# State products of the later pairs, moved directly behind their transposes in a chunked scan fused with a feed-forward block

## The chip, the cores and the metric

The kernel runs on one core of one Trainium2 chip. The metric is the device time of one execution in microseconds (us), the median over several executions. Most executions of one kernel agree within a few tenths of a per cent. In the traces the engines are PE (TensorE's matmuls), PEld (its weight loads), DVE (VectorE), ACT (ScalarE), POOL (GpSimd) and SP (the queue that issues DMAs).

## The reference

Two blocks, one after the other, all in FP32. The first is a chunked state-space scan over 4 batches x 8 heads x 768 positions with head dimension 32 and state dimension 16; the second is a feed-forward block of width 2048 with a learned slope for negative values.

```python
for c in range(nc):                                    # chunks of a sequence
    L = np.exp(cum[..., :, None] - cum[..., None, :]) * causal
    M = np.einsum('bhin,bhjn->bhij', Cc, Bc) * L
    y_intra = np.einsum('bhij,bhjd->bhid', M, xc)
    y_inter = np.einsum('bhin,bhnd->bhid', Cc, state) * decay_to_i[..., None]
    y[:, :, sl] = y_intra + y_inter
    state = decay_full * state + (sum over j of B x x, decayed from j to the end)
...
h = x @ w_in                                           # (3072, 256) @ (256, 2048)
g = np.maximum(h, 0.0) + alpha * np.minimum(h, 0.0)
out = g @ w_out
```

## The kernel before

The 24 chunks of 128 positions are worked as 12 "pairs" and six "groups" of 512 tokens. A generator, `pair(gp)`, does the scan of one pair, and every `yield` ends a step that the caller may place where it likes. Pairs 4 to 11 are the "fine" ones: their steps are laid between the products of the feed-forward block of the group before.

```python
    # pair(gp), fine pairs only; cuts are marked
    tp = ss_tile()                                  # one of 2 PSUM buffers
    ... four transposes of B and C into tp; ACT copies bh; DVE makes cd ...
    yield                                           # step 1
    for w in range(2):
        spread_c(range(2 * w, 2 * w + 2))           # ACT: two scaled copies of C
        half_decays(0, w)                           # DVE: two scans
        yield                                       # steps 2, 3
    ... state products: nk x 2 matmuls in 128x64 tiles; DVE: new state; POOL: mask ...
    yield                                           # step 4
    for w in range(2):
        half_decays(1, w)
        yield                                       # steps 5, 6
    ... two grams (steps 7, 8), then y (step 9) ...
```

The feed-forward block uses a Strassen-like scheme: each "quad" (four per group) has seven half-size products of the first layer and, interleaved, the seven products of the second layer of the quad before. `after(j)` marks 14 places inside a quad. ScalarE and VectorE turn each first-layer result into activations.

```python
    first(A, lambda q: wi[:, q, 0, 0], b11, True);  nc.scalar.copy(out=m1, in_=A);  after(1)
    first(Y, lambda q: s1[:, q], t1, True);         nc.scalar.copy(out=m5, in_=Y);  after(2); after(3)
    first(A, lambda q: s2[:, q], t2);               nc.scalar.copy(out=u2, in_=A);  after(4)
    nc.vector.tensor_tensor(out=Y, in0=Y, in1=u2, op=ALU.add);  after(5)
    first(A, lambda q: wi[:, q, 1, 0], t3)
    ...
    prelu(g12, Y, z, 0);  nc.scalar.copy(out=Y, in_=m1);  prelu(g22, c22, z, 1)
    after(7); after(8); after(9)
    ...
    first(A, lambda q: wi[:, q, 1, 1], t4);  prelu(g21, A, z, 1)   # frees A for the next quad
    after(10); after(11)
    first(Y, lambda q: wi[:, q, 0, 1], b21);  prelu(g11, Y, z, 0)
    ... after(12); after(13); after(14)

# (quad z, place j): which pair's next step goes there, the nearer one (0) or the one after (1)
steps = {(0, 1): 0, (0, 2): 0, (0, 3): 0, (0, 9): 0, (0, 14): 0,
         (1, 1): 0, (1, 2): 0, (1, 5): 0, (1, 9): 0,
         (1, 14): 1, (2, 1): 1, (2, 2): 1, (2, 3): 1, (2, 9): 1, (2, 14): 1,
         (3, 1): 1, (3, 3): 1, (3, 7): 1}
```

In the very first quad there are no second-layer products to interleave; only the last outputs of the phase before stand at its places 3 to 9.

## Time and profile before

| | before |
|---|---|
| median of 3 runs | 404.32 us (404.29 to 404.81) |
| TensorE busy in the profiled run | 378.4 of 402.8 us |
| mean granted TensorE clock | 0.996 of full speed |
| TensorE waits over 0.5 us after 101 us | one for VectorE (1.7), one for ScalarE (1.0) |

One line of the page was not looked at in the prediction and turns out to matter. It gives, for 40 equal slices of the span, the clock that the throttle granted to TensorE, in tenths (9 is nine tenths or more):

```profile
PEclk9999999999999999999999999999999999999998
```

The beginning is not covered: the view counts the clock as whole where it holds no record of it. TensorE's first four transposes, at 7.5 to 8.2 us, take 421 to 474 ns each, the later ones from 19.7 us on 272 to 273, so the clock was probably still low at the start.

### The profile page before, as it was taken

Reading aid. Unit: us, or ns where it says so; the run is one execution under the profiler, and the core shown is the slowest. Engines: PE = TensorE matmul, PEld = TensorE weight load, DVE = VectorE, ACT = ScalarE, POOL = GpSimd, SP = SyncE. Lnnn points to the kernel's source line nnn. Section 1 sums busy time; section 2 is a strip of 40 time slices with the busy share of each in tenths; the row PEclk is TensorE's granted clock in tenths of the full one; section 3 lists DMA queues with packets and bytes.
Section 4 is the critical chain, followed back from the end, with each engine's and each line's share of the span. In section 5 each row is a group of like instructions: output and inputs, shape, how many; then the busy total and the mean of one; then the engine's idle time right before and its main releaser. Section 6 shows DMA issues by size and latency. Waiting matters only on the chain.

```text
span 402.8 us, 6008 instructions
## 1 busy us (share of the span) xinstructions
PE 378.4 (94%) x2131; PEld 294.5 (73%) x2131; DVE 255.4 (63%) x493; ACT 180.2 (45%) x409; POOL 192.6 (48%) x188
## 2 busy tenths in 40 slices
PE   5878979999989999999999999999999999999993
PEld 4454638778858867877868878868878868888883
DVE  5889895691775573675764685674586574355363
ACT  3574823522444534554445544434534534534540
POOL 3164674578174954462453471453471454355511
PEclk9999999999999999999999999999999999999998
DMA  8939997100591430100791100891100200003003
GB/s 208 243 113 223 306 189 160 40 20 0 93 206 52 96 75 2 52 0 2 111 194 35 54 1 2 126 185 29 53 2 4 50 0 2 0 0 55 1 2 52
DMA packets 124126, 30.58 MB, mean 76 GB/s; under 512 B 96880, under 2 KB 120000, under 8 KB 124096
## 3 DMA queue, kind: packets, MB, share of 16 engines
q1 hardware_dynamic: 117792, 29.67, 33.2%
q10 hardware_dynamic: 6304, 0.52, 1.1%
q8 instruction: 17, 0.28, 0.3%
q14 instruction: 13, 0.11, 0.1%
HBM read 26.85 MB, written 3.34 MB: 75 GB/s over the span
## 4 chain that ended last, share of the span: by engine, by line
PE 81%; DVE 9%; ACT 3%; POOL 3%; issue 1%; DMA 1%; DVEq 0%; ACTq 0%; POOLq 0%
PE hp L620 30%; PE bank L595 29%; PE bank L537 6%; PE ss L478 5%; PE hp L524 4%; DVE dec L373 2%; PE ss L501 2%; ACT gt L603 1%; DVE wr L227 1%; DVE dec L483 1%; PE ss L407 1%; PE ss L447 1%; DVE gt L528 1%; POOL gt L663 1%; PE ss L494 1%
## 5 line engine op out<-in xcount | busy, mean ns | idle before, releaser
L663 POOL TENSOR_TENSOR gt<-gt 128x512 f32<-128x512 f32 x58 | 73.6, 1269 | 29.5 <-DVE gt L605 12.8
L595 PE MATMUL bank<-gt,w_out 128*128 128x256 f32 x320 | 82.1, 380 | 0.0
L605 DVE SCALAR_TENSOR_TENSOR gt<-hp,s_mul,gt 128x256 f32<-128x256 f32 x120 | 51.8, 477 | 44.8 <-ACT gt L603 41.7
L603 ACT ACTIVATE gt<-hp,s_alpha 128x256 f32<-128x256 f32 x120 | 50.0, 469 | 62.6 <-PE hp L620 61.3
L595 PEld LDWEIGHTS bank<-gt,w_out 128*128 128x128 f32 x320 | 60.3, 190 | 11.3 <-issue 2.3
L595 PE MATMUL bank<-gt,ws 128*128 128x256 f32 x240 | 58.9, 381 | 0.0
L654 POOL TENSOR_TENSOR gt<-gt 128x512 f32<-128x512 f32 x20 | 25.4, 1270 | 64.4 <-DVE gt L605 64.4
L595 PEld LDWEIGHTS bank<-gt,ws 128*128 128x128 f32 x240 | 45.2, 190 | 6.7 <-issue 0.8
L620 PE MATMUL hp<-xs,w_in 128*128 128x256 f32 x160 | 43.6, 395 | 0.5
L620 PE MATMUL hp<-xT,w_in 128*128 128x256 f32 x160 | 41.5, 382 | 1.7 <-DVE gt L605 1.7
L620 PE MATMUL hp<-xs,ws 128*128 128x256 f32 x160 | 42.3, 387 | 0.0
L379 DVE TENSOR_TENSOR_SCAN dec<-abc,bank 128x256 f32<-128x256 f32 x64 | 39.0, 665 | 0.0
L620 PEld LDWEIGHTS hp<-xs,w_in 128*128 128x128 f32 x160 | 28.1, 189 | 11.9 <-issue 5.9
L620 PEld LDWEIGHTS hp<-xs,ws 128*128 128x128 f32 x160 | 29.1, 190 | 10.1 <-issue 3.7
L620 PEld LDWEIGHTS hp<-xT,w_in 128*128 128x128 f32 x160 | 29.7, 190 | 6.7 <-DVE gt L605 3.1
L483 DVE TENSOR_TENSOR dec<-ss,dec 128x512 f32<-128x512 f32 x40 | 25.6, 682 | 10.5 <-PE ss L478 10.5
L605 DVE SCALAR_TENSOR_TENSOR gt<-c,s_mul,gt 128x256 f32<-128x256 f32 x40 | 17.7, 483 | 23.0 <-ACT gt L603 23.0
L537 PE MATMUL bank<-w_out,gt 128*128 128x256 f32 x128 | 30.4, 379 | 0.0
L524 PE MATMUL hp<-xT,w_in 128*128 128x256 f32 x96 | 25.7, 390 | 4.4 <-DVE gt L528 4.4
L639 DVE TENSOR_TENSOR hp<-hp,u 128x512 f32<-128x512 f32 x20 | 14.0, 700 | 21.7 <-ACT u L637 21.4
L537 PEld LDWEIGHTS bank<-w_out,gt 128*128 128x128 f32 x128 | 24.3, 190 | 3.3
L462 POOL TENSOR_TENSOR sm<-state,bmask 128x256 f32<-128x256 f32 (+1 forms) x12 | 7.7, 643 | 39.1 <-DVE state L458 39.1
(122 smaller groups left out, 539.0 us busy)
## 6 DMA issues: line engine op xcount, KB each, us to landing
abc<-z SPq DMA_DIRECT2D x20, 512.0 KB
raw<-in_moe_w_in_dram SPq DMA_DIRECT2D x8, 512.0 KB
raw<-in_moe_w_out_dram SPq DMA_DIRECT2D x8, 512.0 KB
xt<-in_x_dram SPq DMA_DIRECT2D x24, 128.0 KB
out_dram<-o_sb SPq DMA_DIRECT2D x34, 64.0 KB
nat<-in_B_dram SPq DMA_DIRECT2D x22, 64.0 KB
nat<-in_C_dram SPq DMA_DIRECT2D x22, 64.0 KB
ap<-pf SPq DMA_DIRECT2D x10, 128.0 KB
```

The source lines that it names most:

```text
L379: nc.vector.tensor_tensor_scan(out=dv[:, k, hs], data0=abc[k][:, hs], data1=ident_p[0], initial=0.0, op0=ALU.mult, op1=ALU.add)
L478: nc.tensor.matmul(gram[r].rearrange("p h t -> p (h t)"), bh[rs, k], cz[rs, :, k], start=True, stop=True, tile_position=(64 * r, 0), skip_ ...
L483: nc.vector.tensor_tensor(out=dec[:, k, hs], in0=gram[r], in1=dec[:, k, hs], op=ALU.mult)
L524: nc.tensor.matmul(hp, w_in[:, k, f * P : (f + 1) * P], xts[g][:, k, t0 : t0 + nt], start=(k == 0), stop=(k == KC - 1))
L537: nc.tensor.matmul(pos[0][t // 2][:, t % 2], gt[:, t * Q : (t + 1) * Q], w_out[:, f], start=(f == 0 and t % 2 == 0), stop=(f == NF - 1), s ...
L595: nc.tensor.matmul(ms[g][i][:, h], w, blocks[g, z][n][:, p], start=(q == 0 and h == 0), stop=(q == NQ - 1), skip_group_check=True)
L603: nc.scalar.mul(o[:, p], h[:, p], s_alpha[:, fs[p]])
L605: nc.vector.scalar_tensor_tensor(out=o[:, p], in0=h[:, p], scalar=s_mul[:, fs[p]], in1=o[:, p], op0=ALU.mult, op1=ALU.max)
L620: nc.tensor.matmul(to[:, p], w(2 * z + p), b, start=start and p == 0, stop=True, skip_group_check=True)
L639: nc.vector.tensor_tensor(out=Y, in0=Y, in1=u2, op=ALU.add)
L654: nc.gpsimd.tensor_tensor(out=tc_, in0=g22, in1=g12, op=ALU.subtract)
L663: eng.tensor_tensor(out=o, in0=x0, in1=x1, op=ALU.subtract)
```

## The change

The intent: a fine pair's state products are issued directly behind its transposes, so that the small matmuls of a pair interrupt the block products in one place instead of two. Since that removes one step, each pair has one place fewer: (0,3) goes for the first pair of a group, (2,3) for the second. With (0,3) gone, the first pair's second half scans and spreads land at (0,9), where the state products were. Pair 4's scaled B is prepared explicitly in advance.

```diff
         nc.vector.tensor_tensor(out=cd..., in0=ct, in1=pf, op=ALU.mult)
-        yield
-        if fine:
-            for w in range(2):
-                spread_c(range(2 * w, 2 * w + 2))
-                half_decays(0, w)
-                yield
-        elif gp:
+        if not fine:
+            yield
+        if gp and not fine:
             decays(0)
 ...     # state products, then a yield
         if fine:
-            for w in range(2):
-                half_decays(1, w)
-                yield
+            for k in range(2):
+                for w in range(2):
+                    if k == 0:
+                        spread_c(range(2 * w, 2 * w + 2))
+                    half_decays(k, w)
+                    yield
 ...
+    bns[GC] = pair_loads(GC)
 ...
-    steps = {(0, 1): 0, (0, 2): 0, (0, 3): 0, (0, 9): 0, (0, 14): 0,
+    steps = {(0, 1): 0, (0, 2): 0, (0, 9): 0, (0, 14): 0,
 ...
-             (1, 14): 1, (2, 1): 1, (2, 2): 1, (2, 3): 1, (2, 9): 1, (2, 14): 1,
+             (1, 14): 1, (2, 1): 1, (2, 2): 1, (2, 9): 1, (2, 14): 1,
```

## The prediction

> **What bounds the kernel now.** I read the page first, then the waits of TensorE, then the timeline engine by engine around the places that the change touches. Times in timelines are microseconds from the start of the span; the second column is the length, the last word how many records are merged. An FP32 matmul shows as two records.
>
> ```profile
> PE 378.4 (94%) x2131; PEld 294.5 (73%) x2131; DVE 255.4 (63%) x493; ACT 180.2 (45%) x409; POOL 192.6 (48%) x188
> ```
>
> TensorE is the bound. From 101.3 us on (the second phase, 20 "quads" of seven half-size products each, mixed with the state-space work of the later pairs 4 to 11) it hardly rests: over the stretch from 162.08 to 222.00 its busy time is 59.80 of 59.92 us. The wait view has only two TensorE waits over 0.5 us in that phase, one for a copy of ScalarE that the change leaves alone, and this one:
>
> ```profile
> PE hp L620 <- DVE gt L605: 1.7, 1, 1.7
> ```
>
> It sits at 112.6 to 114.3, at the end of the very first quad, where no block products exist yet to fill the time. So a gain must come from TensorE's own order (mode switches, small stalls), and a loss from ScalarE or VectorE being late for it. The timeline of TensorE in the first quad of the third group shows both places of one pair, transposes (L407) and state products (L447):
>
> ```profile
> 162.08 1.03 PE L620 MATMUL hp<-xT,w_in 128*128 128x256 f32 x4
> 162.94 0.60 PE L407 MATMUL ss<-ident,nat 128*128 128x128 f32 x4
> 163.38 1.03 PE L620 MATMUL hp<-xs,ws 128*128 128x256 f32 x4
> ...
> 165.97 1.03 PE L595 MATMUL bank<-gt,w_out 128*128 128x256 f32 x4
> 167.12 1.10 PE L620 MATMUL hp<-xs,w_in 128*128 128x256 f32 x4
> ...
> 168.92 1.89 PE L595 MATMUL bank<-gt,ws 128*128 128x256 f32 x8
> 170.74 0.66 PE L447 MATMUL ss<-xt,bn 128*64 128x128 f32 x8
> 171.33 1.13 PE L620 MATMUL hp<-xs,w_in 128*128 128x256 f32 x4
> 172.29 1.03 PE L595 MATMUL bank<-gt,w_out 128*128 128x256 f32 x4
> ```
>
> Take starts, since ends overlap. A product (x4) takes 0.86 to the next start. The transposes take 163.38 - 162.94 = 0.44 and cost their neighbours nothing (0.86 before them). The state products take 0.59, and in addition the x8 before them takes 1.82 instead of 1.73 (0.09) and the product after them 0.96 instead of 0.86 (0.10): entry, body and exit are 0.78 us. The step 165.97 to 167.12 is 1.15, a stall of 0.29.
>
> **What the Trainium skill says.** "TensorEngine Tiling (Array Packing)", section Tiling Modes, Key Properties: "Changing tiling mode (not just tile) drains the TensorE". The trace agrees: only the 128*64 state products, not the 128*128 transposes, show the 0.09 and 0.10. The transposes are in the products' own mode, so putting the state products behind them takes no switch away. "TensorE: Matmul & The Clock Gate", section Architectural detail: ScalarE and VectorE take their queue strictly in order, and only TensorE pulls weight loads ahead. The trace agrees: below, ScalarE's copy L637 starts only as the spreads L416 end.
>
> **The change part by part.**
>
> (1) State products move from behind places (0,9) and (2,3) to behind the transposes at (0,1) and (1,14), for 8 pairs. Instructions are the same in kind and number. Per pair the entry of 0.09 may shrink behind a short transpose; exit and body remain. I call the entry there E, between 0 and 0.1, and take 0.05: a gain of 0.04 x 8 = 0.3 us. POOL's scaled B (bn) must now be there earlier: for pair 8 it ends at 221.5 and the transposes start at 222.85, for pair 10 at 281.5 against 282.55, so no wait. Pair 4 gets an early call in the code, but before it ran already at 96.67, right behind the same sums. PSUM's two ss buffers are free then (the copies out of the previous pair's y end some 3 us earlier).
>
> (2) In quad 0 of each group, the second pair of half scans and the second two spreads of C move from (0,3) to (0,9). This matters more, for it moves ScalarE's work from before one copy to before another:
>
> ```profile
> 164.93 1.57 ACT L416 ACTIVATE cz<-ss,par 128x256 f32<-128x256 f32 x4
> 166.36 0.61 ACT L637 COPY u<-hp 128x512 f32<-128x512 f32 x1
> ...
> 172.40 0.35 ACT L685 COPY sa<-bank 128x256 f32<-128x256 f32 x1
> 172.65 0.26 ACT L455 COPY state<-ss 128x128 f32<-128x128 f32 x1
> 172.80 0.85 ACT L603 ACTIVATE gt<-hp,s_alpha 128x256 f32<-128x256 f32 x2
> ```
>
> The gain: L637 frees the bank that the product at 167.12 writes; it starts late by about 0.25 because of four spreads. With two of them gone (0.75 us less) the stall of 0.29 goes, in four groups: 1.15 us at most.
>
> The loss: two spreads (some 0.86 us for a pair, the same length as L603 x2) now stand between L685 and L603 at 172.80. L603 is the first half of the activation whose VectorE half frees the bank of the next quad's first product. Offsets from the quad's start (162.08): the products after the moved state products come E + 0.63 later and 0.2 earlier for the stall, so the first activation is at +7.5 + E instead of +7.09; the chain ScalarE, VectorE (0.10 + 0.88), copy, second activation, L685 carries this on to +11.05 + E; two spreads then bring L603 to +11.85 + E (before: 10.72), its end to 12.7 + E, VectorE's end to 12.8 + 0.88 = 13.68 + E, and the next quad's first product to 13.73 + E. Before, it started at 175.75 - 162.08 = 13.67, and by TensorE's own order it could now start at 13.31 + E. The stall of 0.29 that was removed is thus spent again: 0.06 + E, about +0.1 us for each of groups 2 to 4.
>
> (3) In the first group there are no products to hide this. There ScalarE runs two output copies before the activation (111.53 to 112.58), and the wait of 1.72 is its consequence. The same reckoning puts the activation at 113.7 + E instead of 112.47, VectorE's end at 115.5 instead of 114.23, the next quad at 115.5 instead of 114.28: +1.25 us.
>
> (4) What follows in VectorE. Its next work is a line without a gap up to the first gram multiplication:
>
> ```profile
> 175.15 0.88 DVE L605 SCALAR_TENSOR_TENSOR gt<-hp,s_mul,gt 128x256 f32<-128x256 f32 x2 [0.52 <-ACT gt L603]
> ...
> 177.59 2.41 DVE L379 TENSOR_TENSOR_SCAN dec<-abc,bank 128x256 f32<-128x256 f32 x4
> 179.92 1.26 DVE L483 TENSOR_TENSOR dec<-ss,dec 128x512 f32<-128x512 f32 x2
> ```
>
> L483 ends at 181.18 and frees the banks that the second gram takes at 181.41 (the next x4 of L478): a margin of 0.2. L605 moves from +13.07 to +13.68 + E, so L483 ends 0.65 later while TensorE is only 0.1 later: a stall of about 0.3 us in groups 2, 3 and 4, 0.9 in sum. In the first group L483 ends at 118.66 and the second gram comes at 120.05, so nothing is added.
>
> (5) In quad 2 only the state products move (from (2,3) to (1,14)). ScalarE and TensorE there meet as before; the copy L637 was free of the spreads by 0.8 us and is so by nearly nothing now: 0 to 0.1, taken as 0.
>
> Sum: -0.2 (second pairs' entries; the first pairs' are in the E above) + 0.3 + 1.25 + 0.9 = +2.2 us.
>
> **The rivals.** (a) The merge pays: E is 0, exits shrink too, and ScalarE's delay in (2) stays within the slack. Then it is 4 x 0.29 + 8 x 0.09 = 1.9 us less, 402.4, less whatever (3) costs, about 403.6 with it. For it speaks that the change looks like a deliberate tuning step of a kernel where TensorE is full; against it that the transposes need no switch, and that the delay of L603 follows link by link. (b) The scans or spreads at (0,9) fall where VectorE or ScalarE is already late, and each of the four groups loses some 1.2 us as the first does: 404.3 + 5 = 409. Against it speaks the slack of 0.6 us between VectorE's end and the next quad at 175.75. (c) A transfer or bn on POOL becomes the wait behind the transposes: margins of 1.1 to 1.3 us speak against it; each miss would cost some tenths of a microsecond, giving 405 to 407. (d) All moves lie within the slack: 404.3.
>
> **Range and chances.** The sum gives 406.5. I take 0.4 off for rival (a) and get 406.1. The range reaches from (a) with (3), 403.6, to the sum with larger stalls in (2) and (4), 407.9. Two per cent are 8.1 us: all the stalls in the phase sum to less than half of that, so faster by 2% is all but impossible, and slower by 2% needs (b) and more.
>
> **What would show it.** In the trace after: state products right behind transposes with 0.44 + E + 0.59 between starts and 0.96 for the product after them, the same as before (step 1); 0.86 to 0.95 in place of the 1.15 (step 2, gain); the first quad's wait on VectorE grown from 1.7 to about 2.9 (step 3); a new wait of 0.3 to 0.5 before the second quad's first product, and one of about 0.3 before the second gram, in groups 2 to 4. The prediction is wrong if the state products behind transposes take far less than 0.7, or if the first quad's wait does not grow.

## The result, and the profile after

The changed kernel takes 409.2 us (median of 4 runs, 407.81 to 409.71), the kernel before in the same session 404.56 us (404.29 to 404.95). The ratio is 1.0108, interval 1.0081 to 1.0136. Ratios here are the mean time of one kernel's fast runs over that of the other's in the same rounds, so not quite the ratio of the medians. The loss of some 4.5 us is clear of noise, and the time lies above the predicted range.

The profiled run of after spans 407.7 us at a mean granted clock of 0.979. Its clock line on the page:

```profile
PEclk9999969999989999999999999999999999999998
```

Two slices are low now: around 51 to 61 us and 112 to 122 us; a finer cut shows three stretches at half clock, 18.85 to 22.27, 52.99 to 59.81 and 117.84 to 121.25 us. Each is 3.41 us long or twice that.

The wait that the prediction expected to grow did so, from 1.7 to 3.0 us (waits of TensorE, after):

```profile
PE hp L619 <- DVE gt L604: 3.0, 1, 3.0
```

TensorE's timeline there (start, length, engine, line, number of records; in brackets the idle time before):

```profile
112.52 1.13 PE L619 MATMUL hp<-xT,w_in 128*128 128x256 f32 x4
116.70 1.13 PE L619 MATMUL hp<-xT,w_in 128*128 128x256 f32 x4 [3.05 <-DVE gt L604]
117.67 1.73 PE L619 MATMUL hp<-xs,ws 128*128 128x256 f32 x4
119.33 2.06 PE L477 MATMUL ss<-cz,bh 64*128 64x512 f32 x4
```

The reader should see the last two lines: a product that takes 1.03 us elsewhere takes 1.73, a gram that takes 1.13 takes 2.06. They do the same work at half the clock. The view by stretches confirms it. Its columns are the stretch, its length, then the busy time (and number of instructions) of PE, PEld, DVE, ACT and POOL, the granted clock, the DMA share and GB/s; after:

```profile
114.39:117.80 3.41, 1.10 (x5) 0.99 (x6) 2.64 (x7) 2.07 (x6) 2.29 (x3) 1.00 0.32 91
117.80:121.21 3.41, 3.41 (x9) 1.24 (x7) 1.95 (x4) 1.17 (x2) 3.25 (x3) 0.51 1.13 292
```

TensorE was busy for 1.10 of 3.41 us, and for the next 3.41 us its clock was a half. (The stretches are cut 0.04 us early, hence 0.51; on the exact borders, 114.43 to 117.84, it was busy for 1.14.) In the kernel before, the period that holds most of the wait can be found from its only recorded fall, at 399.26 us at the end: 84 periods of 3.413 us earlier is 112.55, within a few hundredths. There TensorE was busy for 1.69 of 3.41 us and kept its clock:

```profile
112.54:115.95 3.41, 1.69 (x9) 1.43 (x8) 2.84 (x7) 2.01 (x6) 3.09 (x3) 1.00 1.06 334
```

The places that the prediction worked out in the third group, after:

```profile
167.00 0.60 PE L407 MATMUL ss<-ident,nat 128*128 128x128 f32 x4
167.53 0.66 PE L443 MATMUL ss<-xt,bn 128*64 128x128 f32 x8
168.12 1.13 PE L619 MATMUL hp<-xs,ws 128*128 128x256 f32 x4
...
178.66 1.03 PE L594 MATMUL bank<-gt,w_out 128*128 128x256 f32 x4
179.81 1.13 PE L619 MATMUL hp<-xT,w_in 128*128 128x256 f32 x4
...
185.59 1.29 PE L477 MATMUL ss<-cz,bh 64*128 64x512 f32 x4
```

The transposes take 0.53 to the next start instead of 0.44, the state products 0.59 as before: the entry cost came along. The step 178.66 to 179.81 is 1.15, a stall of 0.29 before the next quad's first product, and the second gram has 0.15 more than the usual 1.06 to its next start (186.80). ScalarE's side of the stall, with two spreads (L416) between the copy L684 and the activations L602:

```profile
176.96 0.35 ACT L684 COPY sa<-bank 128x256 f32<-128x256 f32 x1
177.21 0.84 ACT L416 ACTIVATE cz<-ss,par 128x256 f32<-128x256 f32 x2
177.94 1.58 ACT L602 ACTIVATE gt<-hp,s_alpha 128x256 f32<-128x256 f32 x4
```

So the profile of after names three candidates for the loss: the longer waits themselves, the fall of the clock behind the first one, and two falls before 102 us, where both kernels do the same work.

### The profile page after: what moved, and what is told of

It reads as the page before. It is cut to its first block, busy times and chain, and to the rows that moved or that the text cites. A ratio compares the mean times of both kernels' runs of the same rounds, so it can differ in the third digit from the quotient of the medians.

```text
span 407.7 us, 6003 instructions
## 1 busy us (share of the span) xinstructions
PE 383.7 (94%) x2131; PEld 298.7 (73%) x2131; DVE 253.9 (62%) x493; ACT 181.0 (44%) x409; POOL 192.7 (47%) x188
## 4 chain that ended last, share of the span: by engine, by line
PE 80%; DVE 10%; ACT 6%; issue 2%; DMA 1%; POOL 0%; DVEq 0%; ACTq 0%
PE hp L619 30%; PE bank L594 27%; PE bank L536 7%; PE ss L477 5%; PE hp L523 4%; ACT gt L602 2%; PE ss L500 2%; DVE dec L373 2%; DVE gt L604 2%; PE ss L407 1%; DVE dec L482 1%; PE ss L443 1%; ACT cz L416 1%; DVE gt L527 1%; DVE wr L227 1%
## 5 line engine op out<-in xcount | busy, mean ns | idle before, releaser
L602 ACT ACTIVATE gt<-hp,s_alpha 128x256 f32<-128x256 f32 x120 | 49.8, 472 | 60.0 <-PE hp L619 56.6
L619 PE MATMUL hp<-xT,w_in 128*128 128x256 f32 x160 | 42.4, 387 | 3.4 <-DVE gt L604 3.0
L619 PEld LDWEIGHTS hp<-xT,w_in 128*128 128x128 f32 x160 | 29.3, 190 | 10.5 <-DVE gt L604 6.0
L536 PE MATMUL bank<-w_out,gt 128*128 128x256 f32 x128 | 31.6, 390 | 0.0
L523 PE MATMUL hp<-xT,w_in 128*128 128x256 f32 x96 | 27.3, 410 | 2.3 <-DVE gt L527 2.3
L536 PEld LDWEIGHTS bank<-w_out,gt 128*128 128x128 f32 x128 | 25.3, 198 | 3.8
L523 PEld LDWEIGHTS hp<-xT,w_in 128*128 128x128 f32 x96 | 18.3, 201 | 9.9 <-DVE gt L527 6.5
```

What stands on the lines that cost most here:

```text
L523: nc.tensor.matmul(hp, w_in[:, k, f * P : (f + 1) * P], xts[g][:, k, t0 : t0 + nt], start=(k == 0), stop=(k == KC - 1))
L536: nc.tensor.matmul(pos[0][t // 2][:, t % 2], gt[:, t * Q : (t + 1) * Q], w_out[:, f], start=(f == 0 and t % 2 == 0), stop=(f == NF - 1), s ...
L602: nc.scalar.mul(o[:, p], h[:, p], s_alpha[:, fs[p]])
L619: nc.tensor.matmul(to[:, p], w(2 * z + p), b, start=start and p == 0, stop=True, skip_group_check=True)
```

## The experiments

Eleven kernels, each timed in 5 rounds beside the kernel before on the same chip; all gave right results. Theory A says that the longer waits cost their own length, and that the first one also lets the clock fall, for some 1.6 us more; the falls before 102 us are chance. Rival B says that all falls are chance, rival C that the change brings about all of them, and a further rival that the merge itself costs.

A measure that does not depend on what happens before 102 us: in each profiled run, the time from the first transposes of one group to those of the next. Group 1 starts at 102.18 us in the kernel before and contains the first quad; the last column is the first half of group 4.

| profiled run | group 1 | group 2 | group 3 | half of 4 | wait in first quad | clock fell behind it |
|---|---|---|---|---|---|---|
| before | 60.76 | 59.91 | 59.70 | 29.25 | 1.7 | no |
| e2, before again | 60.77 | 59.92 | 59.70 | 29.26 | 1.7 | no |
| after | 63.64 | 60.18 | 59.97 | 29.52 | 3.05 | yes |
| e1, after again | 63.45 | 60.17 | 59.95 | 29.53 | 3.04 | yes |
| e3, pair 4 put back | 63.14 | 60.18 | 59.97 | 29.53 | 2.31 | yes |
| e4, merge alone | 61.49 | 59.85 | 59.63 | 29.20 | 2.31 | no |
| e5, scans alone | 62.92 | 59.70 | 59.48 | 29.20 | 2.45 | yes |
| e6, wait filled | 62.00 | 60.18 | 59.96 | 29.53 | 0.46 | no |
| e9, before with a longer wait | 63.76 | 59.92 | 59.70 | 29.27 | 2.85 | yes |
| e7, better | 59.89 | 59.70 | 59.48 | 29.04 | 1.06 | no |
| e8, scans one place later | 60.55 | 59.70 | 59.48 | 29.04 | 1.7 | no |
| e10, better and filled | 59.90 | 59.70 | 59.47 | 29.05 | 1.1 | no |
| e11, better and merged | 60.30 | 59.62 | 59.42 | 28.98 | 1.3 | no |

The rows repeat to within 0.02 us from one run to the next, except group 1 where the clock fell, so differences of a tenth can be read from it.

### e1_after_again and e2_before_again: both kernels unaltered

> The changed kernel, unaltered, to see whether its slow clock comes back. Theory A (the longer wait of the first quad, 3.05 us, lets the granted clock fall to a half for one stretch of 3.4 us, which costs 1.6 us; and two more such stretches before the changed code are chance): a fall near 118 us in every run, falls before 102 us in some runs only, so times from 407 to 410 with clocks from 0.979 to 0.99. Rival B (the falls are a matter of chance throughout): some runs without any fall, at 406.5 or less and a clock of 0.995. Rival C (the change itself causes the early ones too): falls at 19 and 53 us in every run, all times above 408.5.

> The kernel before, unaltered, as a control with its clocks listed. Theory A: no fall of the clock at the first quad (wait 1.7 us); falls before 102 us possible in some runs by chance, which would show as times of 405.5 to 407 in some runs. If early falls never come in it while they come in every run of the changed kernel, chance is not the reason for them: rival C.

e1 took 408.87 us (six runs, 407.82 to 409.52; clocks 0.978 to 0.995) against 404.84 for the kernel before, ratio 1.0097 (1.008 to 1.0113). Its profiled run had no early fall, and the one in the first quad came again, at 114.82. e2, the control, took 405.26 us (404.23 to 405.53; clocks 0.982 to 0.999), ratio 1.0003, and its profiled run had early falls, at 13.88 and at 51.42 us:

```profile
PEclk9899969999999999999999999999999999999998
```

So rival C falls for the early ones: the kernel before has them too, and the changed kernel need not. They cost less than I expected, up to 1.45 us between two runs of one kernel: the first group begins at 102.78 in e2, 102.18 in before, 103.36 in after, 101.91 in e1. Some cost nothing to be seen: e4, e6 and e8, below, have one or two of them and begin the first group at 101.90, 101.88 and 102.13. Part of the 409.2 of the first session was bad luck of this kind. In none of the ten runs of the changed kernel was the time below 407.8, so rival B's run without a fall did not come.

Within an execution the falls lie whole multiples of one period apart: in after, from 18.85 to 52.99 is 10 x 3.413 us, to 117.84 is 29 x 3.413. From run to run the grid shifts against the kernel's start.

### e3_first_group_back and e4_merge_alone: the scans put back, once for pair 4, once for all

```diff
 # e3, on the changed kernel
-            if nxt < NP and (z, j) in steps:
+            if nxt < NP and ((z, j) in steps or (g, z, j) == (1, 0, 3)) and (g, z, j) != (1, 0, 9):
-                ssm(nxt + steps[z, j])
+                ssm(nxt + steps.get((z, j), 0))
 # e4, on the changed kernel
-    steps = {(0, 1): 0, (0, 2): 0, (0, 9): 0, (0, 14): 0,
+    steps = {(0, 1): 0, (0, 2): 0, (0, 3): 0, (0, 14): 0,
```

> The changed kernel, with the second pair of half scans and spreads of pair 4 alone put back from (0,9) to (0,3). Theory A: the first quad's wait shrinks from 3.05 us to 1.9 to 2.2, no fall of the clock there, so 2.7 us less than the changed kernel: 405.5 where no early fall comes, 406.7 where they come. If the size of the wait has nothing to do with the fall: 1.0 less only, near 408.

> Only the merge: state products behind the transposes, but the half scans and spreads of all first pairs kept at (0,3) instead of (0,9). My account: entry, body and exit of the state products as before (0.78 us), no stall of 0.29 at the next quad nor of 0.25 at the second gram; the stall before the bank that the copy L636 frees stays at about 0.1 to 0.3. So within 0.5 us of the kernel before, 404.3 to 405.0, when the clock doesn't fall. Rival (the merge itself costs): over 406 without a fall.

e3 took 407.51 us (405.87 to 408.49), e4 405.72 us (404.89 to 406.68, ratio 1.0021). My 1.9 to 2.2 for e3's wait was short: it was 2.31 in both, and the clock fell behind it in e3's profiled run and not in e4's. That makes the two a clean pair: the same work in group 1 up to 130 us, the same wait, and the fall as the only difference. TensorE in e3:

```profile
114.87 1.51 PE L619 MATMUL hp<-xT,w_in 128*128 128x256 f32 x4 [2.31 <-DVE gt L604]
116.18 1.91 PE L619 MATMUL hp<-xs,ws 128*128 128x256 f32 x4
```

and in e4:

```profile
114.72 1.13 PE L619 MATMUL hp<-xT,w_in 128*128 128x256 f32 x4 [2.31 <-DVE gt L604]
115.69 1.03 PE L619 MATMUL hp<-xs,ws 128*128 128x256 f32 x4
```

Group 1 is 63.14 against 61.49: a fall costs 1.65 us. Why one fell and the other didn't can be read from the grids. In e3 the whole wait lay in one period (112.07 to 115.48, TensorE busy 1.09 of 3.41). In e4 a border lay inside the wait, at 113.62 (its fall at 52.18 plus 18 periods), and the two periods were busy for 2.20 and 2.31.

The merge alone costs nothing in groups 2 to 4 (0.05 to 0.07 less than before each) and 0.73 in group 1, 0.59 of it by the longer wait. So the rival that the merge itself costs falls for groups 2 to 4 only. In group 1 the merge does cost. Without a fall it comes to 0.55 us net over the four groups, just above the 0.5 I had allowed; in the medians, falls included, e4 lies 0.88 above the kernel before.

### e5_scans_alone: the other half of the change

```diff
 # on the kernel before
-    steps = {(0, 1): 0, (0, 2): 0, (0, 3): 0, (0, 9): 0, (0, 14): 0,
+    steps = {(0, 1): 0, (0, 2): 0, (0, 9): 0, (0, 14): 0,
-                ssm(nxt + steps[z, j])
+                ssm(nxt + steps[z, j], 2 if (z, j) == (0, 9) else 1)
```

> Only the other half of the change: the second half scans and spreads of the first pairs at (0,9), with the state products left there behind block products, so two places as before. My account (the spreads delay the activation that frees the next quad's bank; the merge is worth nothing): the stall of 0.29 at the copy L637 goes, the first quad's wait is 2.3 to 2.9 us, small stalls before the next quad and the second gram: 404.8 to 405.5 without a fall of the clock, 1.65 more with one. Rival (the merge is what costs): 404.3 or less without a fall, the first quad's wait still near 1.7.

405.55 us (404.57 to 407.2), ratio 1.0028. The wait was 2.45 us, as expected, but the small stalls in the later groups were not there: groups 2 and 3 are 0.21 and 0.22 shorter than before, the gain at the copy L637 unspoiled. So in the later groups the two halves do not add. (In the first quad they do: the merge lengthens the wait by 0.59, the scans by 0.73, both together by 1.33.) Alone the merge changes groups 2 and 3 by -0.06 and -0.07 us, alone the scans by -0.21 and -0.22, together they cost 0.27 each. The merge lengthens the quad in front of the first activation and shortens it in front of the one that frees the bank; that takes away just the slack in which the spreads at (0,9) are free. In group 2 the first activation starts 6.88 us after its quad in e5 and 7.59 in after; in e5 VectorE is then done some 0.4 us before TensorE asks for the bank, in after TensorE waits.

### e6_filled_wait: TensorE kept busy in the first wait

```diff
 # on the changed kernel, in after(j)
+            if i == 0 and j == 12:
+                t = bank(2)
+                for _ in range(6):
+                    nc.tensor.matmul(t[:, :HT], wi[:, 0, 0, 0], xts[1][:, 0, :HT], start=True,
+                                     stop=True, skip_group_check=True)
```

> The changed kernel with six idle matmuls (128x256, into a bank that nothing reads before it is begun anew) put into the first quad's wait; the result stays right. Theory A (the idle stretch lets the clock fall): no fall near 115 to 118 us in any run; the wait of VectorE for the next quad ends at the same time; 1.6 us less than the changed kernel: 406 to 407.5, depending on the early falls alone. Rival B (falls there are chance): times as the changed kernel's, 407.8 to 409.5.

406.37 us, and five runs between 406.33 and 406.50, ratio 1.0047 (1.0035 to 1.0059). TensorE:

```profile
112.01 2.75 PE L803 MATMUL bank<-xT,w_in 128*128 128x256 f32 x12
115.22 1.13 PE L619 MATMUL hp<-xT,w_in 128*128 128x256 f32 x4 [0.46 <-DVE gt L604]
116.18 1.03 PE L619 MATMUL hp<-xs,ws 128*128 128x256 f32 x4
117.14 1.13 PE L477 MATMUL ss<-cz,bh 64*128 64x512 f32 x4
```

The next quad still begins when VectorE lets it (115.22; 115.24 in e1, both with the same start of the group within 0.03 us), but everything behind it has its usual length. Work that nobody needs took 1.45 us off group 1 compared with e1. (It is less than 1.65 because e1's fall began 0.42 us before its wait ended.) The scatter of the runs fell from 1.7 us to 0.2; part of that is luck, since the filling does not touch the early falls, of which e6's profiled run has one, at 51.93 us. This is the causal test: the wait was idle time for the throttle, and filling it alone restores the clock.

### e9_longer_wait: the fall without the change

```diff
 # on the kernel before, in after(j)
+            if i == 0 and j == 9:
+                for _ in range(3):
+                    nc.scalar.copy(out=ident_p[0], in_=ident_h[:, :HT])
```

> The kernel before, nothing of the change, with three needless ScalarE copies of 0.38 us ahead of the activation in the first quad, so that its wait grows from 1.7 to 2.8 us. Theory A: 1.1 us from the wait itself in all runs, and a fall of the clock behind it in most, for 1.65 more: 405.5 in runs without, 407.2 in runs with it. Rival B: 405.4 to 406.5 and no more falls than in the kernel before.

407.48 us (407.09 to 408.85), ratio 1.0079 (1.0064 to 1.0095). Nothing of the change is in it, the wait grew by 1.1 us, and the kernel lost over 3 us in its median, with no run below 407.0. Groups 2 to 4 are those of the kernel before. Its wait for ScalarE near 159 us was also 0.3 longer (1.3), which I did not look into, so some 0.3 of its 3.00 us in group 1 is not the first quad's.

### e8_scans_one_later, e7_best, e10_best_filled and e11_best_merged: a version that beats both

If the stall before the bank that L637 frees comes from four spreads ahead of that copy, then placing the second two behind it, at (0,4), should remove it without putting them in front of an activation. The first quad's wait can be cut as well: there ScalarE runs two output copies before the activation that TensorE waits for, and these can come later.

```diff
 # e8, on the kernel before; e7 has this too
-    steps = {(0, 1): 0, (0, 2): 0, (0, 3): 0, (0, 9): 0, (0, 14): 0,
+    steps = {(0, 1): 0, (0, 2): 0, (0, 4): 0, (0, 9): 0, (0, 14): 0,
 # e7 in addition: the end of output(), as a function of its own
-        if f == NF - 1 and half:
+    def output_end():
 ...
+            if i == 0 and j == 12:
+                output_end()
 # e10 in addition: idle matmuls in the first phase, before hidden(0, f, ...)
+            if (n, f) in ((1, 1), (1, 2)):
+                t = bank(0)
+                for _ in range(4 - f):
+                    nc.tensor.matmul(t[:, : 2 * Q], w_in[:, 0, :P], xts[0][:, 0, : 2 * Q],
+                                     start=True, stop=True, skip_group_check=True)
 # e11: e7's two edits on the changed kernel
```

> The kernel before with the second half scans and spreads of the first pairs at (0,4) instead of (0,3), and nothing else. If the stall at the copy L637 is the spreads' doing: 0.2 us less in each of four groups, 0.8 to 1.0 in sum, first quad's wait unchanged at 1.7 or up by 0.3; 403.4 in runs without an early fall of the clock. If it isn't: 404.2.

> A version meant to beat both: the kernel before, with the second half scans and spreads one place later, at (0,4) instead of (0,3), which is behind the copy L637 in ScalarE's order, and with the two output copies of the first quad taken from ScalarE's way until place 12. If the stalls are as I read them: four times 0.25 less at L637, and the first quad's wait shorter by 0.7 to 0.9: 1.8 us less than the kernel before, 402.6. If the delay of the scans only moves elsewhere: 403.5 to 404.3.

> The better version, with five idle matmuls in two waits of the first phase, near 50 and 54 us, where the clock fell in the controls. If those falls come from the idle stretches: no fall near 52 us, times closer together and lower: 402.6 to 403.2 in all runs. If they don't: 402.8 to 404.0 as without them.

> The better version with the merge on top (state products behind the transposes). If the merge is worth nothing in itself and only delays the first activation: the first quad's wait 1.6 instead of 1.1, groups 2 to 4 the same within 0.1: 0.5 to 0.6 us more than the better version without it. Rival (the merge gains once the spreads are out of the way): 0.7 less.

e8 took 404.61 us (403.6 to 404.98), ratio 0.9997: no gain to be seen in times, although every group is 0.21 to 0.22 shorter in its trace, as expected. Early falls probably hid it: its clocks are 0.984 to 0.99, those of the kernel before beside it 0.993 or more in five of eleven runs. That isn't shown, for the only run with a trace has falls at 18.56 and 52.69 us and is the fastest of the six (403.6, near the 403.4 expected). The time alone is inconclusive. e7 took 403.56 us (402.76 to 404.02), ratio 0.9976 (0.9964 to 0.9988): the wait is 1.06 us and groups 1 to 4 are 1.5 us shorter in sum (208.11 against 209.62), with early falls in its profiled run too; I had expected 402.6. e10 took 402.87 us (402.63 to 403.23), ratio 0.9952 (0.9938 to 0.9966), against 404.77 for before. Its page shows no fall until the end:

```profile
PEclk9999999999999999999999999999999999999998
```

With five matmuls whose results nobody reads it has the lowest median of all, though its interval meets that of e7. Groups 1 to 4 take as long as in e7 (208.12 against 208.11); what is gained lies before them, for group 1 begins at 102.15 instead of 103.05. That the matmuls did this by the clock fits its six clocks (0.994 to 0.998), though one profiled run cannot show that such falls never come. e11 took 403.59 us (402.86 to 404.51), ratio 0.9969; in time it cannot be told from e7. The trace shows that the merge then gains 0.06 to 0.08 us in each of groups 2 to 4 and loses 0.41 in the first, a net cost below the 0.5 to 0.6 expected.

## Why the prediction was wrong

The direction was right and most of its sum was good: without falls of the clock the change costs 2.05 us (e6 against before: 1.24 + 0.27 + 0.26 + 0.28 by groups), where the sum said 2.2. Point by point:

1. **State products behind the transposes.** The entry E, taken as 0.05 of a possible 0 to 0.1, measured 0.09 (0.53 instead of 0.44). The drain at a change of tiling mode came along with the move, as the reading of "TensorEngine Tiling (Array Packing)" implied. The merge's own gain is under 0.1 us a group.
2. **The stall at L637 and the next quad.** The stall of 0.29 went and an equal one came before the next quad (179.81 - 178.66 = 1.15). That quad starts 13.67 after its predecessor (166.14 to 179.81), as before: the "0.06 + E" was in fact zero. The product behind the stall then took 0.97 instead of 0.86, 0.11 that I had not counted.
3. **The first quad.** The predicted +1.25 until the next quad begins is measured +1.24 (in after 116.70 - 103.36 = 13.34 from the group's first transposes, before 12.10; the idle stretch itself grew by 1.33). **This is the step that failed**, not by its size but by what it left out: it booked the wait at its own length. TensorE's clock responded to it, and the fall costs 1.45 (e1 against e6) to 1.65 us (e3 against e4) more.
4. **The second gram.** Expected 0.3 in groups 2 to 4, measured 0.15.
5. **Quad 2.** No new wait there, as expected.

One reading in the rivals was off without entering the sum: the slack named under (b), 0.6 us, is 1.12 in the trace (VectorE's half for that bank ends at 174.63, the next quad begins at 175.75).

The sum of the measured terms is 2.05 + 1.5 to 1.65 = 3.5 to 3.7 us; the session of e1 and e2 shows 408.87 - 404.84 = 4.0, the first session 4.6. The rest is within what early falls add by chance (up to 1.45 us in the profiled runs). How much they gave to each session can't be told, since only profiled runs have a trace.

Of the rivals, (a) was right about nothing that matters, and (b)'s figure of 409 came true by luck, for another reason: three of four groups lost only 0.27. The prediction's range was too narrow because none of its rivals had TensorE itself running slower.

The rule was there to be read. "TensorE: Matmul & The Clock Gate", section "What's actually happening", describes a free-running window of 3413 ns after which the clock falls to a half if TensorE was idle. The traces agree on the length (3.41 us), the half and the free running grid. The section "HAM oscillation" puts the rule as no idle gaps above about 3.4 us; here a gap of 2.31 us was enough (e3), so the measurement decides: a gap shorter than the window can do it. At the first quad, the clock fell behind the five windows in which TensorE was busy for 0.73 to 1.14 us, and behind none with 1.69 or more, in all 13 profiles.

Before 102 us busy time alone does not decide. The window before the fall at 18.85 us in after was busy for 1.96 of 3.41 us, and windows just as busy kept their clock in e1 (from 15.83) and in before (from 16.98). A count made on the kept traces afterwards separates them: for each record of a matmul, the columns that it streams (256 for 128x256), times the share of the 128x128 array that its tile covers. From the first record of the clock on, in all 13 profiles, half the clock followed every window with at most 1510 such columns (29 windows), and the whole clock every window with 1582 or more (all the others). The window in after had 1387, the one in e1 1751. Products alone stream 1024 in 0.86 us, some 4060 in a window, so the border lies near 38% of that (an estimate from these numbers). The count fits, but it was chosen after the fact, and no run was made to test it.

## What to carry to other kernels

A wait of the bounding TensorE costs its length only as long as it stays short; look at how it lies against the period in which the granted clock is decided, and reckon with an extra (here 1.45 to 1.65 us) once a window can be mostly idle. Where such a wait can't be removed, matmuls that nobody needs may pay for themselves. And two moves that are each harmless can spend the same slack: merge and scans cost nothing in the later groups one at a time, and 0.27 us a group together.

## What the Trainium skill lacked or had wrong

- "TensorE: Matmul & The Clock Gate" gives the window's length but no share of it that must be busy. Here at the first quad a window with TensorE busy 1.69 of 3.41 us kept the clock (before, 112.54 to 115.95), and those with 1.09 (e3) and 1.14 (after) lost it. Its rule of gaps above about 3.4 us is too lenient for a gap of 2.31 us.
- Beyond a remark on transposes, no page says what counts as busy. In after, the clock fell at 18.85 us although the only wait in the window before was 1.45 us; the matmuls in that window were mostly small ones (128x32 tiles). That a matmul counts by its columns and by the share of the array that its tile covers fits all windows of the 13 profiles (border between 1510 and 1582 columns); it was not tested by a run.
- "TensorEngine Tiling (Array Packing)" says that a change of mode drains the array, without a size. Here 0.09 to 0.10 us on the way in and 0.10 to 0.11 on the way out, behind transposes as behind products.
